# Spreading deferred weight-gradient matmuls over the attention backward of a transformer step, with earlier loads and interleaved dWqkv tiles

## The chip, the cores and the metric

One core of a Trainium2 chip. The metric is the device time of one execution in microseconds (us); medians of several executions are quoted. A profiled execution shows the span of the core, some 2 us below its device time. Engines: PE (matmul; PEld its weight loads), DVE (VectorE), ACT (ScalarE), POOL, SP (issues all DMAs of this kernel, in order). "L396" is a line of the kernel file; lines move between versions.

## The reference

Forward and backward of four residual layers on a sequence of 2048 x 512 in bf16: attention (layer 0), gated GLU (1), attention (2), GLU (3). The outputs are the result and the gradients of x and of five weights, each summed over its two layers.

```python
def _A_ref(x, wqkv, wo):                      # H = 32 heads of 16, W = 8 taps, dilation 2
    q, k, v = ...                             # x @ wqkv
    idx = pos[:, None] - (jnp.arange(8) * 2)[None, :]
    logits = einsum("bhsd,bhswd->bhsw", q, k[idx]) * scale   # masked where idx < 0
    o = einsum("bhsw,bhswd->bhsd", softmax(logits), v[idx])
    return o @ wo
def _B_ref(x, w_gate, w_up, w_down):          # F = 1376
    return (sigmoid(x @ w_gate) * (x @ w_up)) @ w_down
x = x + _A_ref(_layernorm(x), ...); x = x + _B_ref(_layernorm(x), ...)   # twice
# reference(): outputs and jax.vjp of this for grad_out
```

## The kernel before

The backward runs layers 3, 2, 1, 0. Each attention backward (2, then 0) also carries the gate and up weight gradients that the GLU above it left over: 48 tiles of 16 matmuls, called "gu" (ps<-d16c,dxn16d in the trace; 40 tiles have N=256, eight N=96). A compile-time scheduler orders the instructions of each engine, and each engine then executes in order. The stages of one attention backward, cut:

```python
# qk_reduce: dP = dO . v ; then on DVE the softmax backward: rsum, dP - rsum, dS = P * (..)
ph = es2.enter_context(tc.tile_pool(name=f"ab35{l}", bufs=1))      # ONE pool for four buffers
doh = ph.tile(..., tag="b1"); Ph = ph.tile(..., tag="s1")          # shifted dO and P, loaded here
K16 = ph.tile(..., tag="b2"); Kh = ph.tile(..., tag="b3")
# three broadcast passes, each preceded by a lump of three gu chunks (12 tiles):
take = allc[n_done:n_done + 3]
self.glu_dw_gu(dst_["l"], dst_["first"], dst_["dxn"], dst_["p2"], pdw, chunks=take)
self.bcast_acc(Pm, Ph, do16, doh, +1, pw, pacc, sink_v)            # then q, then k
...
n16 = p6.tile([P, NJ, D], BF16, name="n16")                        # after the passes
nc.sync.dma_start(n16[:], self.n_d[l][:])
for blk in range(3):                                               # all 12 dWqkv tiles
    dblk = pw.tile(...); nc.sync.dma_start(dblk[:], self.dqkv_d[:, :, blk * D:(blk + 1) * D])
    for ki in range(KT):
        ...16 matmuls ps += n16.T @ dblk; self.wgrad_out(...)
for j in range(NJ):                                                # "dn loop", 16 iterations
    dj = ...                                                       # load, 12 transposes -> pt
    if b3 == 1: nc.vector.tensor_copy(dTj[...], pt[:])
    else:       nc.scalar.copy(dTj[...], pt[:])
    ...12 matmuls dnps += dTj.T @ wqkvT; self.ln_bwd(...)          # ln_bwd on DVE
# remaining gu tiles
```

A pass has eight row groups (bcast_acc), each eight DVE products and 16 identity matmuls:

```python
for jg in jgs:
    acc0, acc1 = pacc.tile(...), pacc.tile(...)
    for w in range(W):
        pr = product(j0, w)                                        # DVE, 128x1024 bf16
        for jj in range(2):
            nc.tensor.matmul(accs[jj][:], lhsT=self.ident[:], rhs=pr[:, jj, :], ...)
    outs = [sink(j0 + jj, accs[jj]) for jj in range(2)]            # ACT copy, store to dqkv_d
```

A finished gu or dWqkv tile goes through wgrad_out: in layer 2 ("first") ACT copies it and SP stores it to an f32 accumulator; in layer 0 SP loads that accumulator (wg_part), DVE adds (wg_res) and SP stores the output.

## Time and profile before

Median 1846.02 us of four runs (1843.51 to 1846.59). The prediction below shows the lines of its profile. The stages of the two attention backwards, read from the trace of the profiled execution (span 1843.8 us):

| stretch | layer 2, us | layer 0, us |
|---|---|---|
| start: to the first product of the third row group (from the first product in layer 2; from rsum, the end of qk, in layer 0) | 31.4 | 39.5 |
| passes: from there to the end of the last product | 132.1 | 128.0 |
| handover: to the first dWqkv matmul | 18.8 | 19.3 |
| dWqkv and dn: to the last dn matmul | 106.4 | 112.5 |
| tail: to the end | | 12.5 |

How to read it: a stretch is bound by the engine whose work, counted by the pitch of its instructions (the time from one start to the next), fills it. If none does, look for the wait that ends last.

### The profile page before, as it was taken

The page shows a single profiled execution, that of the slowest core. Times are in us where ns is not written, and L with a number is a line of the kernel's source. Part 1 is how long each engine was busy: PE and PEld are TensorE (multiplying, and loading weights), DVE is VectorE, ACT ScalarE, POOL GpSimd, SP SyncE. Part 2 cuts the span into 40 slices and gives each one's busy share as a digit, 9 for nine tenths or more (in the row PEclk, how much of TensorE's full clock was granted, in tenths as well). Part 3 has the DMA queues.
Part 4 walks back from the last instruction along what each step waited for, and adds up shares of the span by engine and source line. Part 5 has one row for each costly group of instructions (what it writes and reads, how often), then busy time and mean ns, then how long its engine had stood idle before and what let it go on. Part 6 is the DMA issues. An engine that isn't in the chain of part 4 may idle for free. (4 is left out here: it accounts for less than half of the span.)

```text
span 1843.8 us, 25729 instructions
## 1 busy us (share of the span) xinstructions
PE 1579.0 (86%) x9706; PEld 869.0 (47%) x9860; DVE 1161.8 (63%) x1973; ACT 573.0 (31%) x1179; POOL 1.1 (0%) x8
## 2 busy tenths in 40 slices
PE   2969899886899969988989998977998978999787
PEld 1534445453344535544565554543553456355344
DVE  5789775488967256752388760454763269897365
ACT  5233766523453533341112221322331100111013
POOL 0000000000000000000000000000000000000000
PEclk9989899998999979999999998998999989999899
DMA  5331855533253585458557557355456854765733
GB/s 177 137 114 56 299 204 150 151 138 126 108 213 143 118 334 192 139 218 282 156 202 246 170 158 229 100 217 178 139 173 224 279 172 142 273 179 153 244 111 114
DMA packets 246764, 329.89 MB, mean 179 GB/s; under 512 B 86480, under 2 KB 207920, under 8 KB 237424
## 3 DMA queue, kind: packets, MB, share of 16 engines
q1 hardware_dynamic: 246640, 328.25, 53.1%
q8 instruction: 77, 1.26, 0.3%
q14 instruction: 47, 0.39, 0.1%
HBM read 188.71 MB, written 139.48 MB: 178 GB/s over the span
## 5 line engine op out<-in xcount | busy, mean ns | idle before, releaser
L396 PE MATMUL acc<-pr,ident 128*128 128x512 bf16 x991 | 282.3, 389 | 36.4 <-DVE pr L379 34.4
L671 PE MATMUL ps<-d16c,dxn16d 128*128 128x256 bf16 (+1 forms) x1536 | 189.7, 263 | 16.3 <-ACT wg_stg L525 10.8
L396 PEld LDWEIGHTS <-ident 128*128 128x128 bf16 x1024 | 98.7, 99 | 158.2 <-issue 52.1
L671 PEld LDWEIGHTS <-dxn16d 128*128 128x128 bf16 x1536 | 137.5, 98 | 60.6 <-issue 19.4
L355 PE MATMUL ps<-prod,ident 128*128 128x256 bf16 x1024 | 126.2, 279 | 28.7 <-DVE prod L233 22.0
L515 DVE SCALAR_TENSOR_TENSOR lnb_junk<-ps,n 128x512 bf16<-128x512 f32 x64 | 44.2, 691 | 155.1 <-PE ps L598 68.2
L355 PEld LDWEIGHTS <-ident 128*128 128x128 bf16 x1024 | 98.3, 100 | 57.2 <-DVE prod L233 23.1
L497 ACT COPY dgs<-pt 128x512 bf16<-128x512 bf16 x128 | 69.6, 588 | 173.3 <-PE pt L491 138.1
L820 PE MATMUL ps<-dblk,n 128*128 128x512 bf16 x376 | 86.2, 390 | 18.8 <-DMA wg_part<-dwqkv_acc 13.4
L585 PE MATMUL ps<-dxT,wdT 128*128 128x512 bf16 (+1 forms) x341 | 83.5, 389 | 16.1 <-DVE dgmT L588 15.1
L458 PE MATMUL gps<-nT,wg 128*128 128x512 bf16 (+1 forms) x341 | 95.6, 386 | 1.9 <-DVE nT L214 1.3
L840 PE MATMUL ps<-wqkvT,dTj 128*128 128x512 bf16 x368 | 87.5, 384 | 5.2 <-DVE dTj L835 4.4
L461 PE MATMUL ups<-nT,wu 128*128 128x512 bf16 (+1 forms) x345 | 91.6, 379 | 0.3
L598 PE MATMUL ps<-wgT,dgmT 128*128 128x512 bf16 (+1 forms) x336 | 89.5, 379 | 0.6
L475 PE MATMUL gps<-wd,hT 128*128 128x512 bf16 (+1 forms) x338 | 85.4, 379 | 0.6
L837 ACT COPY dTj<-pt 128x512 bf16<-128x512 bf16 x64 | 37.4, 585 | 150.3 <-PE pt L833 89.1
L525 ACT ACTIVATE wg_stg<-ps 128x256 f32<-128x256 f32 (+3 forms) x75 | 33.0, 447 | 161.3 <-PE ps L820 36.9
L598 PE MATMUL ps<-wuT,du2T 128*128 128x512 bf16 (+1 forms) x344 | 81.5, 379 | 0.4
L210 PE MATMUL pt<-ident,n16h 128*128 128x128 bf16 x256 | 28.5, 256 | 57.3 <-ACT n16h L200 32.7
L464 DVE SCALAR_TENSOR_TENSOR hT<-tT,ups 128x512 bf16<-128x512 bf16 (+1 forms) x88 | 60.0, 685 | 26.1 <-PE ups L461 21.9
L537 DVE SCALAR_TENSOR_TENSOR wg_res<-ps,wg_part 128x256 bf16<-128x256 f32 (+3 forms) x63 | 28.8, 465 | 71.7 <-PE ps L633 36.2
L463 ACT ACTIVATE tT<-gps 128x512 bf16<-128x512 f32 (+1 forms) x88 | 52.2, 598 | 68.0 <-PE gps L458 66.6
(139 smaller groups left out, 2517.0 us busy)
## 6 DMA issues: line engine op xcount, KB each, us to landing
dgu_d<-dgs SPq DMA_DIRECT2D x64, 320.0 KB, 2.2
d16c<-dgu_d SPq DMA_DIRECT2D x20, 1024.0 KB, 6.3
dqkv_d<-dstg SPq DMA_DIRECT2D x96, 128.0 KB, 1.9
dblk<-dqkv_d SPq DMA_DIRECT2D x6, 2048.0 KB, 10.6
dj<-dqkv_d SPq DMA_DIRECT2D x32, 384.0 KB, 3.1
t_d<-tT SPq DMA_DIRECT2D x20, 512.0 KB, 2.7
m_d<-mT SPq DMA_DIRECT2D x20, 512.0 KB, 2.6
h_d<-hs SPq DMA_DIRECT2D x32, 320.0 KB, 2.9
```

Source lines behind the costliest of these rows:

```text
L355: nc.tensor.matmul(lps[:, 0:HJ * H], lhsT=self.ident[:], rhs=prod[:, :, d * H:(d + 1) * H], start=(d == 0), stop=(d == DH - 1))
L396: nc.tensor.matmul(accs[jj][:], lhsT=self.ident[:], rhs=pr[:, jj, :], start=(w == 0), stop=(w == W - 1))
L458: nc.tensor.matmul(gps[0:fw, :], lhsT=wg[:, k, ft * P:ft * P + fw], rhs=nT[:, k, cs], start=(k == 0), stop=(k == KT - 1))
L461: nc.tensor.matmul(ups[0:fw, :], lhsT=wu[:, k, ft * P:ft * P + fw], rhs=nT[:, k, cs], start=(k == 0), stop=(k == KT - 1))
L464: nc.vector.scalar_tensor_tensor(hT[0:fw, ft, cs], tT[0:fw, cs], 1.0, ups[0:fw, :], ALU.add, ALU.mult)
L475: nc.tensor.matmul(yps[:], lhsT=hT[0:fw, ft, js], rhs=wd[0:fw, ft, :], start=(ft == 0), stop=(ft == FT - 1))
L497: cp(dst[:, g0:g1, :], pt[:, 0:4, :])
L585: nc.tensor.matmul(dhps[0:fw, :], lhsT=wdT[:, k, ft * P:ft * P + fw], rhs=dxT[:, k, cs], start=(k == 0), stop=(k == KT - 1))
L598: nc.tensor.matmul(dnps[:], lhsT=srcT[0:fw, ft, js], rhs=wT[0:fw, ft, :], start=(i_mm == 0), stop=(i_mm == n_mm - 1))
L671: nc.tensor.matmul(ps[:, 0:cw], lhsT=n16[:, j, ki * P:(ki + 1) * P], rhs=d16c[:, j, 0:cw], start=(j == 0), stop=(j == NJ - 1))
L820: nc.tensor.matmul(ps[:], lhsT=n16[:, j, ki * P:(ki + 1) * P], rhs=dblk[:, j, :], start=(j == 0), stop=(j == NJ - 1))
L840: nc.tensor.matmul(dnps[:], lhsT=dTj[:, jt, :], rhs=wqkvT[:, jt, :], start=(jt == 0), stop=(jt == 3 * KT - 1))
```

## The change

Its intent is to give PE the gu matmuls where it waits for DVE, and to have loads in place before they are needed. One gu tile goes into each row group; n is loaded into the place of K during the third pass; the one pool of four buffers becomes four; after two dWqkv tiles the rest alternate with dn iterations; in layer 0 ACT takes over one of the three dTj evictions (copies of transposed blocks out of PSUM) from DVE. The core of the diff:

```diff
+            if filler is not None:
+                filler()                       # in bcast_acc, after the 16 matmuls of a group
...
-                    ph = es2.enter_context(tc.tile_pool(name=f"ab35{l}", bufs=1))
+                    pk = es.enter_context(tc.tile_pool(name=f"ab35pk{l}", bufs=1, reuse_waits="tile"))
+                    pkh = es2.enter_context(tc.tile_pool(name=f"ab35pkh{l}", bufs=1, reuse_waits="tile"))
+                    pss = es2.enter_context(tc.tile_pool(name=f"ab35pss{l}", bufs=1, reuse_waits="tile"))
+                    pdo = es2.enter_context(tc.tile_pool(name=f"ab35pdo{l}", bufs=1, reuse_waits="tile"))
...
-                        take = allc[n_done:n_done + 3]          # before each of the three passes
-                        self.glu_dw_gu(..., chunks=take)
-                    self.bcast_acc(Pm, Ph, do16, doh, +1, pw, pacc, sink_v)
+                    fill(4)
+                    self.bcast_acc(Pm, Ph, do16, doh, +1, pw, pacc, sink_v, filler=fill)
...
+                    n16 = pk.tile([P, NJ, D], BF16, name="n16", tag="b2")     # before the third pass
+                    nc.sync.dma_start(n16[:], self.n_d[l][:])
...
-                n16 = p6.tile([P, NJ, D], BF16, name="n16")
-                nc.sync.dma_start(n16[:], self.n_d[l][:])
-                for blk in range(3): ... 12 dWqkv tiles ...
+                for t in wtiles[0:2]:
+                    dwqkv_tile(*t)
                 for j in range(NJ):
...
-                        if b3 == 1:
+                        if b3 == 1 and l != 0:
                             nc.vector.tensor_copy(dTj[...], pt[:])
...
+                    if wi < len(wtiles):
+                        dwqkv_tile(*wtiles[wi])
+                        wi += 1
+                    if dst_ is not None and l != 0 and j >= 3 and dst_["ems_left"]:
+                        dst_["ems_left"].pop(0)()               # one left-over gu tile
```

More of the change, by code (lines that the diff above doesn't have):

```diff
@@ L357, in qk_reduce, with bcast_acc @@
                 nc.scalar.copy(L[:, w, jb * H:(jb + HJ) * H], lps[:, 0:HJ * H])
-    def bcast_acc(self, Sm, Sh, X16, Xh, direction, pw, pacc, sink, pair=False, sink2=None, reverse=False):
+    def bcast_acc(self, Sm, Sh, X16, Xh, direction, pw, pacc, sink, pair=False, sink2=None, reverse=False, filler=None):
         nc = self.nc
@@ L647, in glu_dw_run @@
             nc.sync.dma_start(buf[:], self.n_d[l][:])
+        if "ems_left" in st:
+            for em in st["ems_left"]:
+                em()
+            return
         done = st.get("done", [])
@@ L653, in gu_chunks, with gu_tile_emitters, em @@
         return [(idx, c0) for idx in (0, 1) for c0 in range(0, F, 256)]
+    def gu_tile_emitters(self, st, psmm):
+        nc = self.nc
+        a = self.aps
+        l, first, n16, p2 = st["l"], st["first"], st["dxn"], st["p2"]
+        specs = ((0, -0.5, self.dwg_acc, "out_4"), (1, 0.5, self.dwu_acc, "out_5"))
+        cache = {}
+        ems = []
+        for (idx, c0) in self.gu_chunks():
+            for ki in range(KT):
+                def em(idx=idx, c0=c0, ki=ki):
+                    (_, sc, acc, oname) = specs[idx]
+                    cw = min(256, F - c0)
+                    if (idx, c0) not in cache:
+                        d16c = p2.tile([P, NJ, 256], BF16, name="d16c")
+                        nc.sync.dma_start(d16c[:, :, 0:cw], self.dgu_d[idx, :, :, c0:c0 + cw])
+                        cache[(idx, c0)] = d16c
+                    d16c = cache[(idx, c0)]
+                    ps = psmm.tile([P, 512], F32, name="ps")
+                    for j in range(NJ):
+                        nc.tensor.matmul(ps[:, 0:cw], lhsT=n16[:, j, ki * P:(ki + 1) * P], rhs=d16c[:, j, 0:cw],
+                                         start=(j == 0), stop=(j == NJ - 1))
+                    out_ap = a[oname][ki * P:(ki + 1) * P, c0:c0 + cw]
+                    self.wgrad_out(ps[:, 0:cw], P, cw, sc, acc[:, ki, c0:c0 + cw], first, p2,
+                                   lambda res, out_ap=out_ap, cw=cw: nc.sync.dma_start(out_ap, res[:, 0:cw]))
+                ems.append(em)
+        return ems
     def glu_dw_gu(self, l, first, n16, p2, psmm, which=(0, 1), chunks=None):
@@ L751, in attn_bwd, with fill @@
                 with ExitStack() as es2:
-                    ph = es2.enter_context(tc.tile_pool(name=f"ab35{l}", bufs=1))
+                    pk = es.enter_context(tc.tile_pool(name=f"ab35pk{l}", bufs=1, reuse_waits="tile"))
+                    pkh = es2.enter_context(tc.tile_pool(name=f"ab35pkh{l}", bufs=1, reuse_waits="tile"))
+                    pss = es2.enter_context(tc.tile_pool(name=f"ab35pss{l}", bufs=1, reuse_waits="tile"))
+                    pdo = es2.enter_context(tc.tile_pool(name=f"ab35pdo{l}", bufs=1, reuse_waits="tile"))
                     pw = es2.enter_context(tc.tile_pool(name=f"ab35w{l}", bufs=4))
                     pacc = es2.enter_context(tc.tile_pool(name=f"ab35pa{l}", bufs=3, space=PSUM))
-                    doh = ph.tile([P, NJ, D], BF16, name="doh", tag="b1")
-                    Ph = ph.tile([P, W, NJ * H], BF16, name="Ph", tag="s1")
+                    ems = self.gu_tile_emitters(dst_, pdw) if (dst_ is not None and (not dst_["with_down"] or dst_.get("down_done"))) else []
+                    def fill(n=1):
+                        for _ in range(n):
+                            if ems:
+                                ems.pop(0)()
+                    doh = pdo.tile([P, NJ, D], BF16, name="doh", tag="b1")
+                    Ph = pss.tile([P, W, NJ * H], BF16, name="Ph", tag="s1")
                     nc.sync.dma_start(doh[:], self.do_d[2:P + 2])
                     nc.sync.dma_start(Ph[:], self.p_d[a][2:P + 2].rearrange("p (w x) -> p w x", w=W))
-                    K16 = ph.tile([P, NJ, D], BF16, name="K16", tag="b2")
-                    Kh = ph.tile([P, NJ, D], BF16, name="Kh", tag="b3")
+                    K16 = pk.tile([P, NJ, D], BF16, name="K16", tag="b2")
+                    Kh = pkh.tile([P, NJ, D], BF16, name="Kh", tag="b3")
                     nc.sync.dma_start(K16[:], self.k_d[a][1:P + 1])
@@ L767, in sink_v @@
                         nc.sync.dma_start(self.dqkv_d[:, j, 2 * D:3 * D], stg[:])
-                    if dst_ is not None and (not dst_["with_down"] or dst_.get("down_done")):
-                        allc = self.gu_chunks()
-                        n_done = len(dst_.setdefault("done", []))
-                        take = allc[n_done:n_done + 3]
-                        self.glu_dw_gu(dst_["l"], dst_["first"], dst_["dxn"], dst_["p2"], pdw, chunks=take)
-                        dst_["done"].extend(take)
-                    self.bcast_acc(Pm, Ph, do16, doh, +1, pw, pacc, sink_v)
-                    Q16 = ph.tile([P, NJ, D], BF16, name="Q16", tag="b1")
-                    dSh = ph.tile([P, W, NJ * H], BF16, name="dSh", tag="s1")
+                    fill(4)
+                    self.bcast_acc(Pm, Ph, do16, doh, +1, pw, pacc, sink_v, filler=fill)
+                    Q16 = pdo.tile([P, NJ, D], BF16, name="Q16", tag="b1")
+                    dSh = pss.tile([P, W, NJ * H], BF16, name="dSh", tag="s1")
                     nc.sync.dma_start(Q16[:], self.q_d[a][1:P + 1])
@@ L783, in sink_q @@
                         nc.sync.dma_start(self.dqkv_d[:, j, 0:D], stg[:])
-                    if dst_ is not None and (not dst_["with_down"] or dst_.get("down_done")):
-                        allc = self.gu_chunks()
-                        n_done = len(dst_.setdefault("done", []))
-                        take = allc[n_done:n_done + 3]
-                        self.glu_dw_gu(dst_["l"], dst_["first"], dst_["dxn"], dst_["p2"], pdw, chunks=take)
-                        dst_["done"].extend(take)
-                    self.bcast_acc(dS16, None, K16, Kh, -1, pw, pacc, sink_q, reverse=True)
-                    Qh = ph.tile([P, NJ, D], BF16, name="Qh", tag="b3")
+                    fill(4)
+                    self.bcast_acc(dS16, None, K16, Kh, -1, pw, pacc, sink_q, reverse=True, filler=fill)
+                    Qh = pkh.tile([P, NJ, D], BF16, name="Qh", tag="b3")
                     nc.sync.dma_start(Qh[:], self.q_d[a][2:P + 2])
+                    n16 = pk.tile([P, NJ, D], BF16, name="n16", tag="b2")
+                    nc.sync.dma_start(n16[:], self.n_d[l][:])
                     def sink_k(j, acc):
@@ L797, in sink_k @@
                         nc.sync.dma_start(self.dqkv_d[:, j, D:2 * D], stg[:])
-                    if dst_ is not None and (not dst_["with_down"] or dst_.get("down_done")):
-                        allc = self.gu_chunks()
-                        n_done = len(dst_.setdefault("done", []))
-                        take = allc[n_done:n_done + 3]
-                        self.glu_dw_gu(dst_["l"], dst_["first"], dst_["dxn"], dst_["p2"], pdw, chunks=take)
-                        dst_["done"].extend(take)
-                    self.bcast_acc(dS16, dSh, Q16, Qh, +1, pw, pacc, sink_k)
+                    fill(4)
+                    self.bcast_acc(dS16, dSh, Q16, Qh, +1, pw, pacc, sink_k, filler=fill)
+                    if dst_ is not None:
+                        dst_["ems_left"] = ems
             with ExitStack() as es2:
@@ L809, in attn_bwd, with dwqkv_tile @@
                 ps6 = es2.enter_context(tc.tile_pool(name=f"abp6{l}", bufs=4, space=PSUM))
-                n16 = p6.tile([P, NJ, D], BF16, name="n16")
-                nc.sync.dma_start(n16[:], self.n_d[l][:])
                 rstd = p6.tile([P, NJ], F32, name="rstd")
                 nc.sync.dma_start(rstd[:], self.rstd_d[l][:])
-                for blk in range(3):
-                    dblk = pw.tile([P, NJ, D], BF16, name="dblk")
-                    nc.sync.dma_start(dblk[:], self.dqkv_d[:, :, blk * D:(blk + 1) * D])
-                    for ki in range(KT):
-                        ps = ps6.tile([P, D], F32, name="ps6")
-                        for j in range(NJ):
-                            nc.tensor.matmul(ps[:], lhsT=n16[:, j, ki * P:(ki + 1) * P], rhs=dblk[:, j, :],
-                                             start=(j == 0), stop=(j == NJ - 1))
-                        out_ap = aps["out_2"][ki * P:(ki + 1) * P, blk * D:(blk + 1) * D]
-                        self.wgrad_out(ps[:], P, D, 1.0, self.dwqkv_acc[:, ki, blk * D:(blk + 1) * D], first, pw,
-                                       lambda res, out_ap=out_ap: nc.sync.dma_start(out_ap, res[:]), perm=True)
+                dblks = {}
+                def dwqkv_tile(blk, ki):
+                    if blk not in dblks:
+                        dblk = pw.tile([P, NJ, D], BF16, name="dblk")
+                        nc.sync.dma_start(dblk[:], self.dqkv_d[:, :, blk * D:(blk + 1) * D])
+                        dblks[blk] = dblk
+                    dblk = dblks[blk]
+                    ps = ps6.tile([P, D], F32, name="ps6")
+                    for j in range(NJ):
+                        nc.tensor.matmul(ps[:], lhsT=n16[:, j, ki * P:(ki + 1) * P], rhs=dblk[:, j, :],
+                                         start=(j == 0), stop=(j == NJ - 1))
+                    out_ap = aps["out_2"][ki * P:(ki + 1) * P, blk * D:(blk + 1) * D]
+                    self.wgrad_out(ps[:], P, D, 1.0, self.dwqkv_acc[:, ki, blk * D:(blk + 1) * D], first, pw,
+                                   lambda res, out_ap=out_ap: nc.sync.dma_start(out_ap, res[:]), perm=True)
+                wtiles = [(blk, ki) for blk in range(3) for ki in range(KT)]
+                for t in wtiles[0:2]:
+                    dwqkv_tile(*t)
+                wi = 2
                 for j in range(NJ):
@@ L842, in attn_bwd @@
                     self.ln_bwd(j, dnps[:], n16, rstd, pw)
+                    if wi < len(wtiles):
[3 more added lines that the diff above has]
+                        dst_["ems_left"].pop(0)()
+                while wi < len(wtiles):
+                    dwqkv_tile(*wtiles[wi])
+                    wi += 1
             if dst_ is not None:
```

## The prediction

> **What bounds the kernel now.** I read the page of the profile first, then the windows of the two stages that the change touches, then who waits for whom there, then the timeline where they hand over. The page:
>
> ```profile
> PE 1579.0 (86%) x9706; PEld 869.0 (47%) x9860; DVE 1161.8 (63%) x1973; ACT 573.0 (31%) x1179; POOL 1.1 (0%) x8
> ...
> PE 14%; DMA 6%; DVE 3%; issue 2%; ACT 1%; SPq 1%; DVEq 0%; ACTq 0%
> ...
> L396 PE MATMUL acc<-pr,ident 128*128 128x512 bf16 x991 | 282.3, 389 | 36.4 <-DVE pr L379 34.4
> ...
> L671 PE MATMUL ps<-d16c,dxn16d 128*128 128x256 bf16 (+1 forms) x1536 | 189.7, 263 | 16.3 <-ACT wg_stg L525 10.8
> ```
>
> PE looks busy for 86%. That is no proof of a bound: in stretches where matmuls follow each other, the distance from start to start is 0.216 us at N=512, 0.109 us at N=256 and 0.042 us at N=96 (medians of the trace), far below the means of 389 and 263 ns. I therefore count matmuls by pitch. The change acts in the attention backward of the two layers, which the trace calls layer 2 (about 930 to 1223 us) and layer 0 (about 1532 to 1844 us). Both have the same stages. The windows view gives, for each stretch, its length, then the busy time of PE, PEld, DVE, ACT and POOL, the clock, the DMA share and GB/s:
>
> ```profile
> 934.60:957.60 23.00, 19.79 (x169) 16.38 (x168) 19.65 (x20) 3.38 (x9) 0.00 (x0) 1.00 0.70 206
> 957.60:966.00 8.40, 5.87 (x33) 3.13 (x33) 4.90 (x9) 1.07 (x2) 0.00 (x0) 1.00 1.02 430
> 966.00:1098.10 132.10, 126.48 (x760) 71.09 (x772) 106.74 (x177) 33.02 (x72) 0.00 (x0) 0.99 0.59 189
> 1098.10:1116.80 18.70, 11.09 (x96) 8.96 (x94) 0.04 (x1) 2.55 (x6) 0.00 (x0) 0.85 0.98 302
> ...
> 1571.50:1699.50 128.00, 124.41 (x677) 62.22 (x688) 113.23 (x199) 23.62 (x44) 0.00 (x0) 0.99 0.61 190
> 1699.50:1718.80 19.30, 5.89 (x52) 4.83 (x51) 1.09 (x4) 1.07 (x2) 0.00 (x0) 0.73 0.83 266
> 1718.80:1762.00 43.20, 42.82 (x191) 19.35 (x196) 22.88 (x12) 0.00 (x0) 0.00 (x0) 0.96 0.69 218
> 1762.00:1768.40 6.40, 2.08 (x20) 1.19 (x17) 5.35 (x4) 1.17 (x2) 0.00 (x0) 0.85 0.26 82
> ```
>
> Rows 1 to 3 and 5 are the broadcast passes (v, q, k), 24 row groups per layer. A group is 8 DVE products (0.68 us each, 0.60 apart, so 4.82 us) and 16 identity matmuls of N=512 (16 x 0.216 = 3.46 us). Left alone a group is DVE-bound and PE has 1.36 us over, room for 12 deferred GLU weight-gradient matmuls of N=256 ("gu" below; 16 make a tile). The kernel before gives gu in lumps: groups with 10 gu still take 4.82 us, groups with 52 to 96 take 8 to 17 us, in which DVE stands still. The waits of DVE in the passes of layer 2 (us in total, times, longest) show that side, and those of PE in layer 0 the other:
>
> ```profile
> DVE pr L379 <- PE acc L396: 13.4, 5, 4.6
> DVE pr L379 <- PE ps L671: 7.8, 2, 4.3
> ...
> DVE pr L379 <- DMA Ph<-p_d: 3.5, 1, 3.5
> ```
>
> ```profile
> PE ps L820 <- DMA wg_part<-dwqkv_acc: 13.4, 1, 13.4
> PE acc L396 <- DVE pr L379: 9.5, 6, 4.3
> PE ps L840 <- DVE dTj L835: 4.4, 1, 4.4
> ```
>
> The 13.4 us is the handover from the passes to dWqkv, in the timeline of layer 0 (start, duration):
>
> ```profile
> 1699.53 0.32 SPq L811 DMA_DIRECT2D n<-n_d  x1
> ...
> 1700.63 1.10 SPq L797 DMA_DIRECT2D dqkv_d<-dstg  x2
> ...
> 1709.82 0.52 SPq L816 DMA_DIRECT2D dblk<-dqkv_d  x1
> ...
> 1718.79 0.59 PE L820 MATMUL ps<-dblk,n 128*128 128x512 bf16 x1 [13.40 <-DMA wg_part<-dwqkv_acc]
> ```
>
> The last stores of dqkv are issued behind the 2 MB load of n, the load of dblk waits 9 us for them, and PE waits for dblk. The wait is named after a smaller load of the same time.
>
> **What the Trainium skill says.** "VectorE: DVE Perf Modes", section "The perf-mode tier table (the rule you actually need)", caps a two-input bf16 operation in SBUF at the 2x tier; the trace agrees: 1024 elements in 0.68 us, so the 4.82 us of a group is a floor. "TensorE: Matmul & The Clock Gate", section "Part 1: The HAM clock gate (the "warmup" mystery)", gives 215.7 ns warm and 426.7 ns cold at N=512 and says that an idle spell takes PE back to half rate; the trace has 0.216, and 0.425 for the first 3.4 us after the 13.4 us gap. So each long gap costs about 1.7 us more than itself. "Perfetto Trace Analysis", section "Optimization Strategy", advises to interleave stretches whose contended engines differ; that is this change.
>
> **The change part by part.** Instruction counts stay the same on all engines (one kind of eviction moves to ACT); what changes is order and waiting. I took the gu per row group from the compiled static order of both kernels.
>
> (1) gu spread over groups. A group costs max(4.82, 3.46 + 0.109 n). Layer 2 before, from the third group on: 6 groups at 4.82 (28.9); then n = 63, 64, 16 and five small ones (50.1); then 83, 64 and six small ones (51.9): 130.9, measured 132.1 (+1.2, kept below). After: six groups up to n = 10 (28.9); then 25, 16, 16, 16, 16, 20, 22, 23 (6.2 + 4 x 5.2 + 5.6 + 5.9 + 6.0 = 44.5); then 63, 0, 32 and five of 16 (10.3 + 4.8 + 6.9 + 26.0 = 48.1): 121.5; the group of 0 follows a PE-bound one, so DVE is ahead there and it goes at PE's pace: -1.4. The start: in the kernel before the first two groups and the softmax backward take 934.6 to 966.0, with 7 us of waits, of which Ph 3.5. Now Ph and doh load during qk (about 20 us earlier, because these pools now release tile by tile), and 144 gu + 32 identity matmuls (15.7 + 6.9 = 22.6 us) lie beside 14.2 us of softmax backward + 16 products (9.6) = 23.8 us of DVE: third group at 958.4. End of the passes: 958.4 + 121.5 - 1.4 + 1.2 = 1079.7 against 1098.1: **-18.4 us**.
>
> Layer 0 before by the same sum: 125.8, measured 128.0 (+2.2). After: 0, 12, 13, 10, 16, 13 (29.4); 80, four of 16, 25, 26, 19 (51.0); 58, 0, 32, five of 16 (47.5): 127.9. The sum is longer than before, but the start is much shorter: the first two groups took 1535.1 to 1571.5 with 9 us of waits (Ph 4.9) and 165 gu; now few gu stand there, the softmax backward starts at 1532.0, ends with 14 products at 1558.6 and two products follow: third group at 1559.8. End: 1559.8 + 127.9 - 1.4 + 2.2 = 1688.5 against 1699.5: **-11.0 us**.
>
> (2) n is loaded in the third pass. At the handover the stores no longer queue behind it; a 1 MB load and one output store still stand in front. I take dblk's issue at 3 to 4 us after the passes' end and 10 us to land (median of issue to landing 10.6, here 8.4 to 9): 13.2 to 14.2 against 18.7 and 19.3. **-4.5 and -6 us**.
>
> (3) dWqkv between the dn iterations. Layer 2: dWqkv and dn took 1116.8 to 1223.0, PE at its pitch nearly throughout; the tiles only change place. But now 128 gu lie in this loop instead of 48 (N=96); a slot of 0.66 us between transposes takes 5 or 6 free, so 1.8 us come on top. Besides, ACT has the dWqkv copies in front of the dTj evictions: some 0.4 us for each of ten iterations, 4.1. **+5.9 us**. Layer 0: the 6.4 us row at 1762.0, where dn waits for a DVE (4.4) that still adds up dWqkv results (2.33 us each), goes, since that addition now lies beside later matmuls and one dTj eviction goes to ACT: **-6.4 us**.
>
> (4) Tail of layer 0: 72 gu instead of 28 of N=96 after the loop, mostly N=96: **+1 us**.
>
> Sum: -18.4 - 4.5 + 5.9 - 11.0 - 6.0 - 6.4 + 1 = -39.4, from 1846.0: 1806.6. I put 1807.
>
> **The rivals.** (a) The gu only move: PE is already the bound in the lumps, so spreading only wins where groups had room, and the lumps (63 and 58 at the third pass, 80 before dWqkv) stay. For: groups of 16 gu cost 5.2, above DVE's 4.82. Against: 13 + 8 us of DVE waits and 36 us of PE idling on products. It would make 1825 to 1835. (b) A DMA wait takes the place of the one removed: dblk still depends on the last stores, SP issues in order, and the 1 MB loads of gu now come in among the stores. For: DMA share 0.59 to 1.02 here. Each wait of 4 us per layer makes 1815 to 1820. (c) Coupling is looser than my sum, products run ahead over several groups: DVE's floor for layer 2 (934.6 + 129.8 = 1064.4) is 15 us below my end, PE's need about 136.5 us is 8 us below it. Then 1790 to 1795. (d) The early Ph and doh loads block SP until the last qk product, and stores behind them come late. Against: SP stands idle there already.
>
> **Range and chances.** The gains at the start, at 6.4 us and at the handovers are nearly sure (about 22 us); spreading is the main unknown (15 to 25), the ACT order of layer 2 the second (0 to 8). 1795 to 1821 holds 8 in 10. The 2% mark is at 1809.1, close above my figure: faster 0.57, same 0.41, slower 0.02.
>
> **What would show it.** Right: groups of 5.2 us in the second and third pass, lumps only at their first group; no DVE wait for Ph; 12 to 14 us from the last product to the first dWqkv matmul; no PE wait of 4.4 for dTj; iterations of dn with a dWqkv tile near 7.4 us (3.92 + 16 x 0.216). Wrong: groups of 6 us or more throughout (PE's pitch is worse when N=256 and N=512 alternate), dblk issued 8 us after the passes, or PE waits for ACT in every iteration of layer 2.

## The result, and the profile after

The changed kernel took 1806.47 us (median of 8 runs, 1803.44 to 1809.47) against 1846.09 us (13 runs) of the kernel before. The ratio is 0.9783, with a 95% interval of 0.9772 to 0.9794. Such ratios are the mean time of one kernel's fast runs over that of the other's of the same rounds, so not quite the ratio of the medians.

The page of the changed kernel (busy time and share of each engine; then the two groups of matmuls that the prediction showed, with busy time, mean ns, and idle time before them):

```profile
PE 1576.4 (87%) x9704; PEld 875.9 (48%) x9860; DVE 1160.8 (64%) x1957; ACT 579.3 (32%) x1195; POOL 1.1 (0%) x8
...
L396 PE MATMUL acc<-pr,ident 128*128 128x512 bf16 x990 | 271.5, 390 | 36.4 <-DVE pr L379 34.7
...
L680 PE MATMUL ps<-d16c,dxn16d 128*128 128x256 bf16 (+1 forms) x1536 | 185.4, 264 | 7.4 <-ACT wg_stg L527 4.5
```

The work is the same (9706 and 9704 matmul records, 1161.8 and 1160.8 us of DVE), in 36 us less of span. PE's share hardly moved, from 86 to 87%: that figure would not have told where the time came from. PE's idle time before the product matmuls (L396) is 36.4 us in both; what fell is its idle time before the gu matmuls (16.3 to 7.4) and before dWqkv (18.8 to 7.0). The windows show where. Each row has the length, then PE, PEld, DVE, ACT and POOL busy, the clock, the DMA share and GB/s. The first three rows are start, passes and handover of layer 2, the last three those of layer 0:

```profile
935.40:959.20 23.80, 22.15 (x164) 16.00 (x165) 23.80 (x29) 4.03 (x10) 0.00 (x0) 1.00 0.87 291
959.20:1081.50 122.30, 119.68 (x728) 68.83 (x740) 107.14 (x177) 32.21 (x69) 0.00 (x0) 1.00 0.66 216
1081.50:1097.50 16.00, 10.95 (x83) 8.60 (x82) 0.00 (x0) 2.22 (x5) 0.00 (x0) 0.89 0.88 276
...
1517.30:1545.30 28.00, 15.59 (x62) 6.48 (x64) 28.00 (x37) 1.59 (x4) 0.00 (x0) 0.70 0.36 140
1545.30:1673.90 128.60, 127.82 (x789) 75.20 (x800) 116.94 (x206) 23.63 (x44) 0.00 (x0) 0.99 0.74 235
1673.90:1687.40 13.50, 9.46 (x84) 8.00 (x83) 1.31 (x4) 1.07 (x2) 0.00 (x0) 0.93 0.81 244
```

Both starts are now DVE-bound: 23.80 of 23.80 us and 28.00 of 28.00 us of DVE. In layer 0 PE is busy for only 15.6 us there. The waits of DVE in start and passes of layer 2 show the rest (us in total, times, longest). The line for Ph is gone, and the last line, which stood at 7.2 us before, is nearly so; its releaser "remote" is not explained by the view:

```profile
DVE pr L379 <- PE acc L396: 9.0, 7, 5.1
DVE pr L379 <- PE ps L680: 5.7, 5, 2.2
DVE pr L379 <- remote: 0.5, 1, 0.5
```

The handover of layer 0 in the timeline (start, duration), to be held against the four lines of the prediction:

```profile
1675.06 0.81 SPq L831 DMA_DIRECT2D dqkv_d<-dstg  x2
...
1678.47 0.53 SPq L848 DMA_DIRECT2D dblk<-dqkv_d  x1
...
1687.36 0.59 PE L853 MATMUL ps<-dblk,n 128*128 128x512 bf16 x1 [4.04 <-issue]
```

The stores now clear in 3.4 us (9.2 before), and PE idles 4.0 us instead of 13.4, since 80 gu matmuls fill most of the wait. The label "issue" says that the profile names no releaser; dblk, issued 8.9 us earlier, is the likely one (its loads land in 8.6 us at the least).

Stage by stage, before, as the prediction works out, and after (us, from traces):

| stretch | layer 2: before | predicted | after | layer 0: before | predicted | after |
|---|---|---|---|---|---|---|
| start | 31.4 | 23.8 | 23.8 | 39.5 | 27.8 | 28.0 |
| passes | 132.1 | 121.3 | 122.3 | 128.0 | 128.7 | 128.6 |
| handover | 18.8 | 14.2 | 16.0 | 19.3 | 13.3 | 13.5 |
| dWqkv and dn | 106.4 | 112.3 | 109.7 | 112.5 | 106.1 | 106.7 |
| tail | | | | 12.5 | 13.5 | 13.4 |

The differences sum to 38.5 us. The spans differ by 36.4, because the changed kernel's profiled run entered layer 2 0.8 us later and spent 1.4 us more between the two layers, where nothing was changed.

### The profile page after: what moved, and what is told of

Read it like the earlier page. It is cut to its first block, busy times and chain, and to the rows that moved or that the text cites. A ratio compares the mean times of both kernels' runs of the same rounds, so it can differ in the third digit from the quotient of the medians.

```text
span 1807.5 us, 25681 instructions
## 1 busy us (share of the span) xinstructions
PE 1576.4 (87%) x9704; PEld 875.9 (48%) x9860; DVE 1160.8 (64%) x1957; ACT 579.3 (32%) x1195; POOL 1.1 (0%) x8
## 5 line engine op out<-in xcount | busy, mean ns | idle before, releaser
L396 PE MATMUL acc<-pr,ident 128*128 128x512 bf16 x990 | 271.5, 390 | 36.4 <-DVE pr L379 34.7
L680 PE MATMUL ps<-d16c,dxn16d 128*128 128x256 bf16 (+1 forms) x1536 | 185.4, 264 | 7.4 <-ACT wg_stg L527 4.5
L396 PEld LDWEIGHTS <-ident 128*128 128x128 bf16 x1024 | 100.3, 99 | 149.7 <-issue 46.8
L587 PE MATMUL ps<-dxT,wdT 128*128 128x512 bf16 (+1 forms) x341 | 83.7, 389 | 16.9 <-DVE dgmT L590 15.9
L875 ACT COPY dTj<-pt 128x512 bf16<-128x512 bf16 x80 | 45.0, 586 | 95.1 <-PE pt L871 95.1
L539 DVE SCALAR_TENSOR_TENSOR wg_res<-ps,wg_part 128x256 bf16<-128x256 f32 (+3 forms) x63 | 29.3, 472 | 65.3 <-PE ps L635 37.2
## 6 DMA issues: line engine op xcount, KB each, us to landing
dqkv_d<-dstg SPq DMA_DIRECT2D x96, 128.0 KB, 2.3
```

The source lines that it names most:

```text
L587: nc.tensor.matmul(dhps[0:fw, :], lhsT=wdT[:, k, ft * P:ft * P + fw], rhs=dxT[:, k, cs], start=(k == 0), stop=(k == KT - 1))
L680: nc.tensor.matmul(ps[:, 0:cw], lhsT=n16[:, j, ki * P:(ki + 1) * P], rhs=d16c[:, j, 0:cw], start=(j == 0), stop=(j == NJ - 1))
L875: nc.scalar.copy(dTj[:, b3 * KT:(b3 + 1) * KT, :], pt[:])
```

## The experiments

Twelve kernels ran beside the kernel before (medians of it: 1845.7 to 1845.9 us). All results were correct. All but the tenth are edits of the changed kernel, and "control" is that kernel run again. First all results together, with medians in us and the stages from their traces (start, passes, handover, dWqkv and dn):

| run | median | ratio, 95% interval | layer 2 | layer 0 |
|---|---|---|---|---|
| before | 1846.1 | 1 | 31.4, 132.1, 18.8, 106.4 | 39.5, 128.0, 19.3, 112.5 |
| 1 control | 1807.3 | 0.979 (0.977 to 0.981) | 23.7, 122.3, 16.3, 109.5 | 28.0, 128.7, 13.4, 106.8 |
| 2 dWqkv first | 1810.5 | 0.980 (0.977 to 0.982) | 23.7, 121.5, 15.9, 110.3 | 28.0, 129.3, 13.4, 110.0 |
| 3 eviction on DVE | 1813.8 | 0.983 (0.980 to 0.985) | 23.7, 121.5, 15.8, 110.7 | 28.0, 129.3, 13.3, 114.4 |
| 4 both | 1811.4 | 0.980 (0.978 to 0.983) | 23.7, 122.3, 16.2, 110.3 | 28.0, 129.4, 13.3, 114.4 |
| 5 one pool | 1827.3 | 0.990 (0.988 to 0.992) | 35.4, 121.2, 16.2, 109.6 | 39.6, 127.7, 13.2, 104.4 |
| 6 n late, first try | 1809.0 | 0.980 (0.978 to 0.982) | 23.7, 121.6, 16.1, 110.5 | 28.0, 129.8, 13.1, 107.1 |
| 7 lumps | 1817.0 | 0.984 (0.983 to 0.986) | 27.6, 131.0, 13.3, 107.8 | 30.3, 131.1, 13.9, 105.9 |
| 8 eight in front | 1801.2 | 0.976 (0.974 to 0.977) | 23.8, 122.3, 16.0, 109.7 | 29.3, 121.1, 13.3, 106.1 |
| 9 n late | 1815.2 | 0.984 (0.982 to 0.987) | 23.7, 122.9, 20.8, 107.9 | 28.0, 129.2, 18.3, 106.9 |
| 10 split alone | 1839.5 | 0.998 (0.996 to 1.000) | 28.6, 132.3, 18.3, 107.1 | 30.5, 133.6, 18.8, 112.7 |
| 11 early v block | 1784.7 | 0.967 (0.965 to 0.969) | 23.7, 121.6, 2.2, 116.6 | 31.3, 125.1, 2.2, 104.5 |
| 12 twelve in front | 1804.0 | 0.977 (0.975 to 0.980) | 23.8, 122.3, 16.1, 110.7 | 31.6, 124.1, 13.0, 105.8 |

Where an edit touches one stage, that stage of the trace tells more than the medians, which scatter by 2 to 4 us. The stages scatter too, by their clock: the loop of layer 2, the same code in runs 1 and 12, took 109.5 and 110.7 us. By the clock records of the traces PE stood at half the granted clock for 3.0 and 5.4 us of it, and half of that difference is the 1.2 us. Below, "at half clock" is this figure. Counts of gu in a stage are of weight-load records, of which none is missing.

### 1. Control

> The changed kernel itself again, as the control for the three kernels beside it: 0.978 of the kernel before (1803 to 1809 us).

Measured: 1807.3 us. The gain repeats, and the stages repeat within 0.3 us of the profile above.

### 2 to 4. What interleaving and the moved eviction do

Run 2 has all twelve dWqkv tiles before the loop:

```diff
-                for t in wtiles[0:2]:
+                for t in wtiles[0:12]:
-                wi = 2
+                wi = 12
```

> All 12 dWqkv tiles stand before the dn loop again; the eviction of dTj in layer 0 stays on ACT. Theory: the 6.4 us of part (3) were one wait, of the first dn matmuls for a dTj eviction that stood on DVE behind four additions of 2.33 us; ACT alone already takes it away, so interleaving is not needed for it: the stretch from the first dWqkv matmul to the last dn matmul of layer 0 stays within 2 us of 106.7, and the time within 3 us of the control. Rival: interleaving itself made the gain, because the additions need matmuls to lie beside: that stretch grows by about 6 us, and the time is 5 to 8 us above the control.

Run 3 leaves the tiles interleaved and puts the eviction back on DVE in layer 0:

```diff
-                        if b3 == 1 and l != 0:
+                        if b3 == 1:
```

> Interleaving stays; the dTj eviction of layer 0 is on DVE again. In the static order it now stands directly behind an addition of 2.33 us in each of ten iterations. Theory: that addition starts when its dWqkv tile ends, and the first dn matmuls need dTj some 2.4 us later, so PE waits 0.3 to 1 us in each of ten iterations: 3 to 10 us above the control. Rival: transposes and slots hide it, and the eviction's engine is indifferent once the tiles are interleaved: within 2 us of the control.

Run 4 has both edits.

> Both parts undone: all dWqkv tiles before the loop, dTj of layer 0 on DVE. Theory: the wait of the kernel before is back once, with PE waiting 4 to 5 us for a dTj of DVE and about 6 us in all: 5 to 8 us above the control. Rival: in the new order of gu tiles the wait is gone anyway: within 2 us of the control.

Measured: the time of runs 2 and 4 lies 3 and 4 us above the control, with overlapping intervals, so by the clock alone these two would be unclear. The stage "dWqkv and dn" of layer 0 is clear: 106.8 in the control, 110.0, 114.4 and 114.4 in runs 2, 3 and 4. The wait of PE behind each of the three, in this order:

```profile
PE pt L871 <- DMA dj<-dqkv_d: 2.6, 1, 2.6
```

```profile
PE ps L878 <- DVE dTj L873: 5.4, 11, 0.5
```

```profile
PE ps L878 <- DVE dTj L873: 4.4, 1, 4.4
```

Run 4 restores the 4.4 us wait of the kernel before. It costs more than itself: for the two iterations after it, 5.4 and 5.5 us long instead of 3.9, the granted clock was 0.50. With the eviction on ACT alone (run 2) both are gone, and 2.6 us of waiting for a dj load remain. With interleaving alone (run 3) the wait comes back as eleven waits of half a microsecond: in the trace each eviction then stands behind one addition instead of behind several. So interleaving without the eviction on ACT is worth nothing here (114.4 both ways); the eviction alone is worth 4.4 us and both 7.6. My theory for run 2 (within 2 us) was off by 1.2 us: I had not seen the dj load. My theory for run 3 held. That for run 4 held in the stage (7.6 us longer), not in the time: 4 us above the control, where 5 to 8 were expected.

### 5. One pool again

```diff
-                    pkh = es2.enter_context(tc.tile_pool(name=f"ab35pkh{l}", bufs=1, reuse_waits="tile"))
-                    pss = es2.enter_context(tc.tile_pool(name=f"ab35pss{l}", bufs=1, reuse_waits="tile"))
-                    pdo = es2.enter_context(tc.tile_pool(name=f"ab35pdo{l}", bufs=1, reuse_waits="tile"))
+                    pkh = es2.enter_context(tc.tile_pool(name=f"ab35ph{l}", bufs=1))
+                    pss = pkh
+                    pdo = pkh
```

> doh, Ph, Kh and their successors come from one pool again, as in the kernel before; the rest is the changed kernel. The load of Ph is then released only by the last DVE operation of the softmax backward (dS), not by the end of qk. (Setting the release option of the pools back alone compiles to the same program, so my prediction named the wrong part of the edit: it is the split in four pools that counts.) Theory: Ph lands 12 to 14 us after dS, the third row group starts about 7 us later in layer 2 and 8 us later in layer 0, of which some 4 us come back in layer 0 because 48 gu matmuls fill the wait: 8 to 13 us above the control of 1807. Rival: PE carries these groups and the early load is worth under 4 us.

Measured: 1827.3 us, 20 us above the control, more than I expected. The start is 11.7 us longer in layer 2 and 11.6 us in layer 0. Its timeline in layer 0 (start, duration; in brackets the idle time and its releaser):

```profile
1547.49 4.42 DVE L782 TENSOR_TENSOR dS<-Pm,dP 128x4096 bf16<-128x4096 bf16 x1
...
1552.78 0.91 SPq L800 DMA_DIRECT2D Ph<-p_d  x1
...
1564.43 0.69 DVE L379 TENSOR_TENSOR pr<-doh,Ph 128x1024 bf16<-128x1024 bf16 x1 [6.98 <-DMA Ph<-p_d]
```

Ph is issued 0.9 us after dS ends; in the changed kernel it is issued 26 us before dS ends. There it lands in 4.9 us; here the first product that needs it starts 11.7 us after the issue, with loads of doh, K and Kh beside it. The loss is 11.7 and not 7 to 8 because the products that need no Ph had moved up: in the kernel before, 5 and 7 products had started when dS ended, here 12 and 15, so that DVE reaches the first product that needs Ph sooner and waits longer for it. In layer 0, where 48 gu matmuls fill the wait, I expected 4 us back. The passes are only 1.0 us shorter than in the control. The stage dWqkv and dn is 2.4 us shorter, but with the same 59 gu in both: the control ran 5.0 us of it at half clock and run 5 none. Run 5 joins three of the four buffers; K, whose place n takes, keeps its own pool.

### 6 and 9. n loaded after the passes

```diff
-                    n16 = pk.tile([P, NJ, D], BF16, name="n16", tag="b2")      # before the third pass
-                    nc.sync.dma_start(n16[:], self.n_d[l][:])
...
+                    n16 = pk.tile([P, NJ, D], BF16, name="n16", tag="b2")      # after it
+                    nc.sync.dma_start(n16[:], self.n_d[l][:])
```

> n is loaded after the third pass again. Theory: its 2 MB stand in front of the last stores and of dblk; the stretch from the last product to the first dWqkv matmul is back at 18.7 and 19.3 us (16.0 and 13.5 in the changed kernel): 7 to 10 us above the control of 1807. Rival: dblk's own load from the last stores sets the start anyway: within 3 us of the control.

Measured: 1809.0 us, handovers of 16.1 and 13.1 us. This looks like the rival's result, but the trace says that nothing was tested: n was issued at 1025.7 and 1634.9 us, still in the third pass. The source order does not fix the order of issue; the scheduler put it back as soon as K's buffer was free. Run 9 gives n a pool of its own that exists only after the passes:

```diff
-                    pk = es.enter_context(...)
+                    pk = es2.enter_context(...)
...
+                n16 = p6.tile([P, NJ, D], BF16, name="n16")
+                nc.sync.dma_start(n16[:], self.n_d[l][:])
```

> The run before with n after the passes did not test it: the compiled order put its load back into the third pass. Here n has its own pool after the passes, as in the kernel before, and the compiled order has its load just ahead of the last stores. Theory (n's 2 MB delay the last stores and dblk): the stretch from the last product to the first dWqkv matmul is 18 to 20 us in both layers instead of 16 and 13.5: 5 to 9 us above the control of 1807. Rival: within 3 us, the handover got shorter for another reason.

Measured: 1815.2 us, 8 us above the control; handovers of 20.8 and 18.3 us, 4.5 and 4.9 us longer. In layer 0:

```profile
1673.16 0.32 SPq L840 DMA_DIRECT2D n<-n_d  x1
...
1676.45 1.04 SPq L829 DMA_DIRECT2D dqkv_d<-dstg  x2
...
1682.68 0.53 SPq L848 DMA_DIRECT2D dblk<-dqkv_d  x1
```

From the last stores to the issue of dblk it takes 6.2 us, against 3.4 in the changed kernel; the stores themselves go out 3.3 us after the last product instead of 1.2. The theory holds.

### 7. Lumps

```diff
-                    fill(4)
-                    self.bcast_acc(..., filler=fill)
+                    fill(12)
+                    self.bcast_acc(...)                     # in all three passes
```

> The same 36 gu tiles per layer in the three passes, but twelve in front of each pass instead of four in front and one per group; all else is the changed kernel. By the group sum (the larger of 4.82 and 3.46 + 0.109 n) the passes of layer 2 take 129.2 instead of 121.5 and those of layer 0 134.1 instead of 128.0; four tiles more come into the passes of layer 2 out of the dn loop, which gives back 3 to 4 us there, and the tail of layer 0 is some 2 us shorter. Theory (spreading is worth what the sum says): 5 to 11 us above the control of 1807. Rival (gu only move, PE is the bound either way): within 3 us.

Measured: 1817.0 us, 9.7 us above the control. The passes of layer 2 took 131.0 us (sum: 129.2), those of layer 0 131.1 (sum: 134.1); the starts are 3.9 and 2.3 us longer too, which I had not counted. What was to come back did so in part: dWqkv and dn of layer 2 is 1.7 us shorter and its handover 3.0. So in layer 2 the group sum is right to 2 us, in layer 0 it was 3 us too pessimistic. The passes alone do not isolate spreading, for the edit also brings gu into them: start and passes of layer 2 have 581 instead of 520, 6.6 us of PE at their pitch. All stages of a layer, with the tail, have the same gu in both kernels, and there run 7 loses 7.9 us in layer 2 and 3.1 in layer 0 (6.7 and 4.1 if the loops' time at half clock is allowed for). So the rival, that gu only move, falls.

### 8 and 12. More tiles in front of the first pass of layer 0

```diff
-                    fill(4)                                  # first pass
+                    fill(8 if l == 0 else 4)                 # run 12: 12 if l == 0
...
-                    fill(4)                                  # second pass
+                    fill(0 if l == 0 else 4)
```

> Changed kernel, but in layer 0 eight tiles in front of the first pass and none in front of the second: PE stands idle some 12 us beside the softmax backward of layer 0, and the second pass starts with a lump of 80 gu matmuls that takes 12.3 us. Theory: the lump goes (12.3 to about 5 us) and the 64 matmuls cost nothing where they now stand: 5 to 8 us below the control of 1807. Rival: their transfers collide with the early loads of Ph and doh, or the products wait for PE at the start: under 3 us of gain.

Measured: 1801.2 us, 6.1 us below the control. The second pass of layer 0, before (control) and then with eight tiles in front, in the windows view:

```profile
1575.50:1624.90 49.40, 49.08 (x339) 30.30 (x343) 43.15 (x79) 8.68 (x16) 0.00 (x0) 1.00 0.69 212
```

```profile
1577.80:1619.30 41.50, 41.05 (x271) 23.65 (x275) 41.41 (x74) 8.68 (x16) 0.00 (x0) 1.00 0.69 217
```

The pass is 7.9 us shorter and now DVE-bound (41.4 of 41.5 us). The 64 matmuls cost 1.3 us where they now stand, and not on PE: the start is still all DVE (29.3 of 29.3 us, with four more instructions of DVE, as many as tiles were moved).

> The changed kernel with twelve tiles in front of the first pass of layer 0 and none in front of the second; nothing else. The compiled order leaves no gu for the tail of layer 0 (72 in the changed kernel). Theory: the lump and the tail go, 1793 to 1799 us. Rival: the start of layer 0 becomes PE-bound and takes back what the tail gives: 1800 to 1804, as with eight tiles.

Measured: 1804.0 us, not better than with eight (1801.2); the intervals overlap. The start took 31.6 us instead of 29.3 and the passes 124.1 instead of 121.1; the tail, without gu, took 12.2 us instead of 13.4 in the control. The rival's time came out, at its edge, but not its reason. The start did not become PE-bound:

```profile
1518.20:1549.80 31.60, 24.25 (x158) 16.80 (x161) 30.41 (x43) 1.69 (x4) 0.00 (x0) 0.89 0.76 249
```

DVE is busy for 30.4 of 31.6 us, PE for 24.3. And the passes have 29 more gu than with eight tiles (413, 384), 3.2 us at their pitch, which is about what they lost.

### 10. The kernel before with the pools split, nothing else

```diff
-                    ph = es2.enter_context(tc.tile_pool(name=f"ab35{l}", bufs=1))
+                    pk = es2.enter_context(tc.tile_pool(name=f"ab35pk{l}", bufs=1))
+                    pkh = ...; pss = ...; pdo = ...          # doh, Ph, K16, Kh and successors from these
```

> The kernel before with one part of the change alone: the single pool of doh, Ph, K and Kh split in four. In the compiled order Ph and doh are then loaded at the end of qk. Theory: the start of the passes alone is worth 7 to 11 us per layer, lumps or not: 16 to 20 us below the kernel before (1826 to 1830 us, ratio 0.989 to 0.991). Rival: the lumps in front of the first pass keep PE busy over the wait anyway, so that the early load pays only with spread gu: under 6 us.

Measured: 1839.5 us, 6 us below the kernel before by the medians, 4.4 by the ratio (0.998, 0.996 to 1.000). That is the rival's range by the one and just outside it by the other; the theory's 16 to 20 us are not reached. The windows show start and passes of layer 0:

```profile
1531.80:1559.20 27.40, 18.94 (x125) 12.73 (x126) 27.03 (x36) 1.07 (x2) 0.00 (x0) 0.94 0.81 255
1559.20:1692.80 133.60, 129.88 (x748) 68.92 (x759) 114.79 (x202) 23.72 (x44) 0.00 (x0) 1.00 0.59 188
```

The start is 9.0 us shorter (30.5 from the end of qk, against 39.5), but the passes are 5.6 us longer. In the kernel before, 176 gu matmuls ran in this start and filled the wait for Ph; now 110 do, and the other 66 stand in the passes (402 instead of 336), 7.2 us of PE at their pitch. In layer 2 only 2.8 us are won at the start, with PE busy for 23.9 of 28.6 us there. The same split is worth 20 us when the gu are spread (run 5 against the control). The rest of the change without the split is worth 19 us (run 5 against before), the split alone 6; together they are worth 39. About 14 us exist only when both are there. As run 5 leaves K's pool apart, "the rest" is not quite the change without its split.

### 11. The v block of dWqkv loaded early

The first pass finishes the v third of dqkv, yet its dWqkv tiles come after the last stores of all. Here dblk for v is loaded during the second pass into the place of dO, which no one reads after the first pass; twelve tiles stand in front in layer 0, as in run 12:

```diff
-            do16 = big.tile([P, NJ, D], BF16, name="do16")
+            do16 = big.tile([P, NJ, D], BF16, name="do16", tag="dob")
...
+                    dblkv = big.tile([P, NJ, D], BF16, name="dblk", tag="dob")      # before the third pass
+                    nc.sync.dma_start(dblkv[:], self.dqkv_d[:, :, 2 * D:3 * D])
...
-                dblks = {}
-                wtiles = [(blk, ki) for blk in range(3) for ki in range(KT)]
-                for t in wtiles[0:2]:
+                dblks = {2: dblkv}
+                wtiles = [(blk, ki) for blk in (2, 0, 1) for ki in range(KT)]
+                for t in wtiles[0:4]:
```

> Attempt at a better kernel: twelve tiles in front of the first pass of layer 0 and none in front of the second, and the v block of dWqkv is loaded during the second pass into the place of dO, so that its four tiles (13.8 us) stand ready when the passes end. Theory: the 5 to 7 us of PE idling at each handover go, and the clock does not fall: 1788 to 1797 us. Rival: the gu matmuls that filled the handover (80 became 20) cost the same time in the dn loop and the tail: no better than the kernel beside it.

Measured: 1784.7 us, ratio 0.967, 19 us below the kernel beside it (run 12) and better than I expected. The handover of layer 0:

```profile
1663.68 1.91 PE L680 MATMUL ps<-d16c,dxn16d 128*128 128x256 bf16 x16
...
1665.42 13.98 PE L856 MATMUL ps<-dblk,n 128*128 128x512 bf16 x63
```

64 dWqkv matmuls (one record is missing) run through in 13.98 us, at 0.218 each. From the last product to the first dn matmul (1663.2 to 1680.6) PE is busy for 17.3 of 17.4 us at a granted clock of 1.00. Both handovers shrink to 2.2 us. In layer 2 the gu matmuls that had filled the handover come back in the dn loop (116.6 instead of 110.7), in layer 0 most go to the tail (59 of 80; 21 to the loop), which is 0.8 us longer, and the loop is shorter (104.5 instead of 105.8). I had expected 5 to 7 us per layer. It is 8.0 in layer 2 (16.1 - 2.2 - 5.9) and 11.3 in layer 0 (13.0 - 2.2 + 1.3 - 0.8). A part is the clock: the loops of run 12 ran 5.4 and 3.1 us at half clock, those of run 11 none, worth 2.7 and 1.5 us. The surplus in layer 0 also includes the waits of the loop, of which run 12 had a 3.0 us one for dblk and eleven for ACT's dTj (5.4 us together), and run 11 neither.

## Why the prediction was right

The time was 1806.5 against 1807 predicted. It matters whether the steps were right, or only their sum.

**Starts.** Predicted 23.8 and 27.8 us, measured 23.8 and 28.0. Run 5 shows that the early load of Ph is the cause: without it the starts are 35.4 and 39.6. One statement was wrong: I put the early load down to the pools releasing tile by tile. With that option taken out, the compiled order of SP with its waits, of PE and of DVE is the same (compared, not run). Run 10, which splits the pools without that option, issues Ph 25 us before dS ends in layer 0, while joining the pools (run 5) moves the load behind dS. It is the split that counts. Why a shared pool waits for dS (probably its place in memory overlaps that of dP) is not shown by a run.

**Passes.** Predicted 121.3 and 128.7, measured 122.3 and 128.6. The group rule, the larger of 4.82 and 3.46 + 0.109 n, was slightly low: groups with 16 gu took 5.36 us instead of 5.20. Run 7 confirms that spreading counts, by 7.9 us in layer 2 and 3.1 in layer 0. One argument did not hold: the 36 us of PE idling on products, held against rival (a), stayed at 36.4.

**Handovers.** Layer 0: 13.3 predicted, 13.5 measured. Layer 2: 14.2 against 16.0. There dblk went out 5.4 us after the passes, not 3 to 4, with a store of gu results ahead of it on SP, and the first dWqkv matmul came 10.6 us later, not 10. This is rival (b), at a size of 1.8 us. PE also waited 2.8 us for ACT to free a gu tile (ACT itself had waited 5.4 for the store of an earlier one), but idled 2.3 us more after that, so this did not set the end. Run 9 shows that n's place matters by 4.5 and 4.9 us. The stages fell by 2.8 and 5.8; no run separates the rest.

**dWqkv and dn.** In layer 2 I predicted +5.9 as 1.8 for more gu and 4.1 for ACT's order. The sum came out at +3.3, and both terms were wrong. Run 4 has the order of the kernel before with the new gu, at 110.3: the gu cost 3.9 (0.5 of it because more of the loop, 5.4 against 4.5 us, ran at half clock). Of the 128 gu now there, 64 have N=256: at their pitch 7.6 us more than the 48 of N=96 before, of which half or more found room. ACT's order costs next to nothing: interleaved, run 3 took 110.7, with the same 5.4 us at half clock, so 0.4 instead of 4.1; iterations with a dWqkv tile take 7.46 us, and 3.92 + 3.46 is 7.38. Two errors, 2.1 too little and 3.7 too much, partly cancelled, and 1.0 us came from a clock that was at half for 3.4 us instead of 5.4. That the stage missed by only 2.6 us is luck in part.

In layer 0, -5.8 measured against -6.4. Against run 4 (114.4) the eviction on ACT makes 4.4 and interleaving on top of it 3.2; I had named both parts without telling them apart. But run 4 lies 1.9 above the kernel before (112.5): it ran 12.7 us at half clock, the kernel before 10.1, which makes 1.3 of the 1.9; the rest is not shown. So the parts gained 7.6, and that 6.4 came close is luck in part.

**Tail.** +0.9 against +1.

The signed errors were: starts +0.2, passes +0.9, handovers +2.0, loops -2.0, tail -0.1 (measured minus predicted, us). Together 1.0. The prediction took each long gap to cost some 1.7 us more by a slow start of PE. The skill's clock rule ("TensorE: Matmul & The Clock Gate", "Part 1: The HAM clock gate (the "warmup" mystery)") shows in the traces, but not as a fixed price of a gap. First the start of dWqkv in layer 0 of the changed kernel, after 4.0 us of idle time, then the same in run 5, after 3.8 us (the clock is the number before the last two):

```profile
1687.40:1692.20 4.80, 4.58 (x11) 1.68 (x13) 0.00 (x0) 0.00 (x0) 0.00 (x0) 0.50 1.06 373
```

```profile
1705.90:1712.40 6.50, 6.43 (x30) 2.96 (x32) 2.33 (x1) 0.00 (x0) 0.00 (x0) 1.00 1.07 367
```

After 4.0 us the matmuls stood 0.43 us apart for 4.8 us (for 3.3 us after the 13.4 before); after 3.8 us they ran at 0.216 at once. In layer 2 of the changed kernel 2.8 us of idle time were enough for a clock of 0.50. The same section calls the window in which activity is counted free-running, which would let gaps of like length end differently; no run here tests it. Run 11, without the gap, kept 1.00 in both handovers.

Of the rivals, (a) holds as a part: 69 gu left start and passes of layer 2 and 11 its handover for the dn loop, where they cost 3.9 us. (c) and (d) did not show.

## What to carry to other kernels

Count the work of a stretch by the pitch of its instructions, group by group, as the larger of two engines, and calibrate the sum on the kernel before: here that predicted starts and passes within 1.0 us. The handovers were taken from a load's issue and landing (within 1.8), and the loop of layer 2 missed by 2.6, with terms off by more. A filler pays only where the engine it fills really waits; before judging two parts of a change by themselves, ask whether one takes away the wait that the other was to fill (6 and 19 us apart, 39 together). And look, at each handover through memory, for a part of the data that was complete long before: loading that part early was worth more than reordering what waits.

## What the Trainium skill lacked or had wrong

- "TensorE: Matmul & The Clock Gate", Part 1: right in its pitches (0.216 and 0.43 us at N=512). It does not say what it costs to mix widths: 16 matmuls of N=512 with 16 of N=256 took 5.36 us per group, where their pitches sum to 5.20. (No run shows that the mixing is what costs the 0.16.)
- "Perfetto Trace Analysis", "Optimization Strategy": its advice to interleave regimes held, but it does not say that spreading and early loads depend on each other: 6 us for the split alone, 19 us for the rest alone, 39 for both.
- No page that I read treats how buffers are grouped in pools as something that decides when a transfer may go out: joining doh, Ph and Kh in one pool cost 11.7 and 11.6 us at the start of the two layers (20 us of the time).
